# Linear attention and two feed-forward layers on one core: k and v on 128 rows in four steps and one, two attention banks in turn, q loaded a pair ahead

## The chip, the cores and the metric

The kernel runs on one core of a Trainium2 chip. The metric is the device time of one execution in microseconds (us). Before the change the median of three runs is 881.73 us (879.92 to 881.73).

## The reference, cut to what matters

q, k and v have 4 batches, 8 heads, 576 tokens and a head size of 64. Each head's kv is a sum over its 576 tokens; q times kv is normalised per token; then come two layers of the same form (512 to 2048 to 512) with different activations. All is float32.

```python
def _attn_ref(q, k, v, g_norm):
    kv = np.einsum('bhsd,bhse->bhde', k, v)
    out = np.einsum('bhsd,bhde->bhse', q, kv)
    rms = np.sqrt(np.mean(out * out, axis=-1, keepdims=True) + 1e-06)
    return (out / rms * g_norm).astype(np.float32)

def reference(...):
    x = attn_out.transpose(0, 2, 1, 3).reshape(2304, 512)
    h = x @ w_in;  sp = log1p(exp(h));  x = (h * np.tanh(sp)) @ w_out          # layer 1: mish
    h = x @ w_in2; x = (np.maximum(h, 0) + alpha * np.minimum(h, 0)) @ w_out2  # layer 2: prelu
    return x
```

## The kernel before, in words

**Blocks and slots.** The 2304 tokens are cut into five blocks (512, 256, 512, 512, 512). Each block goes through layer 1 and later through layer 2; the 2048 inner features are cut into 16 tiles, so the program has 2 x 5 x 16 = 160 slots, each for one block and one tile. In slot s TensorE does mm1(s), the product x times w_in for that tile, into a bank "h" of PSUM, and mm2(s-4), the product of the activated tile of four slots before with w_out, into four banks acc0 to acc3 that add up over the 16 tiles. Each product of two float32 values is made as three products of a high and a low part (`three`, L118 to L120): high with high, high with low, low with high. In between, mish (L458, ScalarE) or prelu (L466, L468, VectorE) reads bank h, and g_split (L451, L452) cuts the result into its parts. PSUM has eight banks; three of them are for h (`ps_h`), one is for the attention ("at").

**Weights.** The weights lie in memory as 64-bit numbers. A tile of w_in (w1) or w_out (w2) is loaded into a ring of three stage buffers "ws" (L328, L331), ScalarE scales its high words (L339), VectorE puts a float32 together from the bits (L345, L346, L349), ScalarE casts it to the high part (L384), and VectorE takes the low part (L388). In layer 1 this goes on in slots 4 to 19, one tile of w1 and one of w2 a slot.

**Attention.** Heads go in pairs, four pairs a block. The attention of block 0 stands at the start in an order written out by hand (`START`). That of the other blocks is spread over the slots before they are needed, in "hooks": hook 2s comes behind mm1(s), hook 2s+1 at the end of slot s. `WHEN[i] = (h0, step, dk, do, dm, db)` gives the places for block i: at h0 + p * step the transposes of q of pair p (t_pe, bank "tps", copied by ScalarE), dk later the sum over tokens of k times v (kv_pe, bank "kvps", where the next batch is needed), do later q times kv (o_pe, bank "ops"); after the last pair, dm later, the mean square (ms_pe) and four parts of an inverse square root on VectorE whose last result is "yr"; and from db later on, one a hook, four products that spread yr over the rows (b_pe, bank "bps", L293), each followed by VectorE's product (L299, into "qT") and the split into the parts xh and xl of x (L309, L314). Blocks 1 to 4 need kv of batches 1, 2 and 3 besides batch 0; a new batch's k and v are loaded pair by pair with q.

**kv.** k and v of a pair are loaded as 96 rows: row p holds tokens 6p to 6p+5 of both heads (`KVJ` = 6). kv_pe runs six steps, each with one product of 96 rows for each head.

**Order.** Up to slot 19 the order on every engine is the order of the program text; from slot 20 on only TensorE's is, and a scheduler places the rest. All loads are issued by SyncE (SP), in one queue. A load is called in `pre` of a slot: weights two slots and attention some slots ahead of use; in one slot the weights of the list come first. SyncE stops at a load whose buffer isn't free yet.

Of the kernel before, what the change touches and what calls it, by code (L numbers as in the profile page):

```python
# [9 lines left out]
F32 = mybir.dt.float32  # L10
# [14 lines left out]
P = 128  # L25
# [1 line left out]
EPS = 1e-6  # L27
SHIFT = 28
MAGIC = 0x5F3759DF
KVJ = 6  # L30
BLOCKS = (512, 256, 512, 512, 512)
ORDER2 = (0, 2, 3, 4, 1)
SPREAD = 4
EARLY = 4
WHEN = {1: (8, 3, 1, 2, 3, 4), 2: (-4, 4, 1, 2, 3, 7), 3: (0, 5, 1, 2, 4, 5), 4: (0, 5, 1, 2, 4, 5)}
MANUAL = 20
FIRST = "p0 c0 p1 c1 p2 p3 c2 c3 w4 u0 w5 u1".split()
START = """
# [8 lines left out]
def attn_moe_moe2(  # L47
# [27 lines left out]
    nc = tc.nc  # L75
    B, H, S, D = q.shape
# [20 lines left out]
    kvp = ctx.enter_context(tc.tile_pool(name="kvp", bufs=1))  # L97
    dp = ctx.enter_context(tc.tile_pool(name="dp", bufs=1, space=bass.MemoryType.DRAM))
    ps_acc = ctx.enter_context(tc.tile_pool(name="ps_acc", bufs=1, space=bass.MemoryType.PSUM))
    ps_h = ctx.enter_context(tc.tile_pool(name="ps_h", bufs=3, space=bass.MemoryType.PSUM))  # L100
    ps_a = ctx.enter_context(tc.tile_pool(name="ps_a", bufs=1, space=bass.MemoryType.PSUM))

    ident = const.tile([P, P], F32, name="ident")
# [39 lines left out]
    def load_kv(b, p):
        R = S // KVJ
        for nm, src in (("k", k), ("v", v)):
            cols = 2 * KVJ * D
            t = room(nm, F32, cols) if b == 0 else kvp.tile([P, cols], F32, tag=nm, name=nm)
            t = t.rearrange("p (h j d) -> p h j d", h=2, j=KVJ)
            nc.sync.dma_start(
                out=t[:R], in_=src[b, 2 * p : 2 * p + 2, :, :].rearrange("h (p j) d -> p h j d", j=KVJ)  # L150
            )
            kvt[nm, b, p] = t[:R]

    def parts(i):

# [8 lines left out]
    def load_q(i, p):  # L164
# [9 lines left out]
                )  # L174
        qt[i, p] = t

    def bank(tag, nm):
        pool = {"h": ps_h, "at": ps_a}.get(tag, ps_acc)
        return pool.tile([P, 512], F32, tag=tag, name=nm)

    def kv_pe(b, p, tag="at"):
        kt, vt = kvt.pop(("k", b, p)), kvt.pop(("v", b, p))
        ps = bank(tag, "kvps")
        for j in range(KVJ):
            for h in range(2):
                hs = slice(h * D, (h + 1) * D)
                nc.tensor.matmul(ps[hs, hs], kt[:, h, j, :], vt[:, h, j, :], start=(j == 0), stop=(j == KVJ - 1))  # L187
        at["kv", b, p] = ps

    def kv_of(b, p):  # L190
# [10 lines left out]
    def t_pe(i, p, tag="at"):  # L201
        t = qt.pop((i, p))
        ps = bank(tag, "tps")
        for c in range(BLOCKS[i] // P):
            cs = slice(c * P, (c + 1) * P)
            if i == 0:
                for h in range(2):
                    nc.tensor.matmul(ps[h * D : (h + 1) * D, cs], t[:, h, c, :], ident, start=True, stop=True)
            else:
                nc.tensor.transpose(ps[:, cs], t[:, :, c, :], ident)  # L210
        at["t", i, p] = ps
# [27 lines left out]
        nc.scalar.activation(out=sq, in_=ps, func=AF.Square)  # L239

    def m_pe(p):
        at["m", p] = bank("at", "mps")
        nc.tensor.matmul(at["m", p], ones_bd, at["o", 0, p][1], start=True, stop=True)

    def m_ev(p):
        y = at["o", 0, p][1]
        u = at["u", p] = buf(True, p, ap, TM, F32, "u", "u")
        nc.scalar.activation(
# [161 lines left out]
    hps, gs, gt, acc = {}, {}, {}, {}  # L410

    def at_slot(kk):
        b = order[kk // NJ]
        return kk // NS, b, kk % NJ, BLOCKS[b % NB]

    def mm1(kk, chunks=range(4)):
        L, i, j, T = at_slot(kk)
        if chunks[0] == 0:
            hps[kk] = bank("acc3" if kk == 3 else "h", "h")
        ps = hps[kk]  # L420
        wh, wl = w1[L, j]
# [80 lines left out]
    pre, hook, mid, fin, last = ({} for _ in range(5))  # L502

    def add(d, s, f, *a):
        d.setdefault(s, []).append((f, a))
# [2 lines left out]
        for f, a in d.pop(s, []):  # L508
            f(*a)

    early_w = [({"w": 1, "u": 2}[n[0]], int(n[1:])) for n in FIRST if n[0] in "wu"]
    for j in range(NJ):
        if j >= EARLY and (1, j) not in early_w:
            add(pre, j - 2, load_w, 0, 1, j)
            add(mid, j - 2, w_begin, 0, 1, j)
        if (2, j) not in early_w:
            add(pre, j + 2, load_w, 0, 2, j)
            add(last, j + 2, w_begin, 0, 2, j)
            add(mid, j + 3, w_end)
        s = NS - NJ + 2 + SPREAD * j // 4  # L520
        add(pre, s, load_w, 1, 1, j)
        add(fin, s + 2, prep_w, 1, 1, j)
        s = NS + j
        add(pre, s - 1, load_w, 1, 2, j)
        add(fin, s + 1, prep_w, 1, 2, j)
    new_kv = {1: 1, 2: 2, 3: 3}
    for i in range(1, NB):
        h0, step, dk, do, dm, db = WHEN[i]
        h0 += (i - 1) * 2 * NJ
        for p in range(NP):  # L530
            h = h0 + p * step
            before = max((h - step + dk) // 2 + 1 if p else h // 2 - 2, EARLY)
            add(pre, before, load_q, i, p)
            add(hook, h, t_pe, i, p)
            add(hook, h, t_ev, i, p)
            if i in new_kv:
                add(pre, before, load_kv, new_kv[i], p)
                add(hook, h + dk, kv_pe, new_kv[i], p)
                add(hook, h + dk, kv_ev, new_kv[i], p)
            add(hook, h + do, o_pe, i, p)  # L540
            add(hook, h + do, o_ev, i, p)
        h += dm
        add(hook, h, ms_pe, i)
        for part in range(4):
            add(hook, h + part, rsqrt_ev, i, part)
        for p in range(NP):
            add(hook, h + db + p, b_pe, i, p)
            add(hook, h + db + p, b_ev, i, p)
    for pos in range(NB, 2 * NB):
# [24 lines left out]
    def warm(n):  # L574
# [30 lines left out]
    with tc.manual_schedule():  # L605
        nc.scalar.preload_act_table_set("abs_reciprocal_sqrt_and_small")
        for n in FIRST:
            if n[0] == "p":
                load_kv(0, int(n[1]))
                load_q(0, int(n[1]))  # L610
            else:
                load_w(0, code[n[0]], int(n[1:]), True)
            if n == "p1":
                for h in range(2):
                    nc.sync.dma_start(out=gcol[h * D : (h + 1) * D, :], in_=g_norm.rearrange("(p o) -> p o", o=1))
# [12 lines left out]
        for p in range(NP):  # L628
            for h in range(2):
# [49 lines left out]
```

## Time and profile before

| | before |
|---|---|
| median of three runs | 881.73 us |
| the profiled execution | 880.43 us |
| its span, first to last instruction | 878.7 us |
| TensorE matmul (PE), busy | 857.0 us (98%) |
| TensorE weight load (PEld), busy | 705.9 us (80%) |
| VectorE (DVE), busy | 443.0 us (50%) |
| ScalarE (ACT), busy | 283.1 us (32%) |
| mean granted clock of TensorE | 0.996 |

The profile shows one execution; its span is 1.7 us shorter than the execution's own time, for what lies before the first and after the last instruction. Busy shares are means over the whole span. In 40 slices of the span TensorE shows 7 to 9 tenths in the first six and then 9 in all but the last; VectorE shows 5 to 9 in the first six and otherwise mostly 1 to 7. The name in front of a `<-` in a row is the tile that is written, those behind it are read. "SPq" is the queue of SyncE's loads.

### The profile page before, as it was taken

The numbers are of one execution on the slowest core, as the hardware profiler recorded it, in microseconds if no ns is written. First come the engines' busy times: TensorE is split into PE (matmuls) and PEld (weight loads), VectorE is DVE, ScalarE is ACT, GpSimd is POOL, SyncE is SP. The second block draws the span as 40 slices with busy tenths as digits, with TensorE's granted clock in tenths as the row PEclk, the third lists the DMA queues.
The fourth block names the chain that finished last, engine by engine and source line by source line (L and its number), as shares of the span: only waits on it lengthen the run. The fifth ranks groups of instructions, "written<-read, shape, count | busy, mean of one in ns | idle before, by whom it ended". The sixth has DMA issues, their size and how long they took to land.

```text
span 878.7 us, 10843 instructions
## 1 busy us (share of the span) xinstructions
PE 857.0 (98%) x4396; PEld 705.9 (80%) x4396; DVE 443.0 (50%) x752; ACT 283.1 (32%) x521; POOL 1.4 (0%) x11
## 2 busy tenths in 40 slices
PE   7988889999999999999999999999999999999998
PEld 5667668898878877888888888888888888888897
DVE  5986864531144131625777796453344334433453
ACT  4765445434323242334554342121112111111111
POOL 0000000000000000000000000000000000000000
PEclk9999999999999999999999999999999999999999
DMA  9746644203100040004632440030002000100010
GB/s 232 221 141 199 178 140 114 88 1 101 41 13 1 12 132 1 1 24 134 202 119 96 144 163 29 0 97 1 1 0 84 1 1 0 61 1 1 1 48 24
DMA packets 50754, 62.57 MB, mean 71 GB/s; under 512 B 19729, under 2 KB 41233, under 8 KB 50705
## 3 DMA queue, kind: packets, MB, share of 16 engines
q1 hardware_dynamic: 50704, 61.89, 23.6%
q8 instruction: 34, 0.56, 0.3%
q14 instruction: 16, 0.12, 0.1%
HBM read 52.44 MB, written 9.44 MB: 70 GB/s over the span
## 4 chain that ended last, share of the span: by engine, by line
PE 92%; DVE 3%; DMA 2%; ACT 1%; SPq 1%; issue 0%; DVEq 0%
PE acc L118 15%; PE acc L120 15%; PE acc L119 15%; PE h L118 15%; PE h L120 14%; PE h L119 14%; PE ops L225 2%; PE kvps L187 1%; DMA q<-in_q_dram 1%; DMA v<-in_v_dram 1%; PE tps L210 1%; DVE wf L346 1%; DVE wf L349 1%; DVE w L388 1%; PE msps L267 0%
## 5 line engine op out<-in xcount | busy, mean ns | idle before, releaser
L452 DVE TENSOR_TENSOR gl<-n,gh 128x512 fp32r<-128x512 f32 (+1 forms) x160 | 102.0, 637 | 327.8 <-ACT gh L451 327.2
L451 ACT CAST gh<-n 128x512 fp32r<-128x512 f32 (+1 forms) x160 | 92.4, 578 | 382.3 <-PE acc L119 249.1
L118 PE MATMUL h<-xh,w 128*128 128x512 f32 (+1 forms) x480 | 179.2, 373 | 0.0
L120 PE MATMUL h<-xh,w 128*128 128x512 f32 (+1 forms) x480 | 176.9, 369 | 0.1
L119 PE MATMUL h<-xl,w 128*128 128x512 f32 (+1 forms) x480 | 176.7, 368 | 0.0
L118 PE MATMUL acc<-gh,w 128*128 128x512 f32 (+1 forms) x320 | 122.1, 382 | 1.4 <-ACT n L458 1.4
L120 PE MATMUL acc<-gh,w 128*128 128x512 f32 (+1 forms) x320 | 119.5, 373 | 0.0
L119 PE MATMUL acc<-gl,w 128*128 128x512 f32 (+1 forms) x320 | 119.2, 372 | 0.0
L118 PE MATMUL acc<-w,gh 128*128 128x512 f32 x288 | 112.2, 390 | 0.0
L119 PE MATMUL acc<-w,gh 128*128 128x512 f32 x288 | 112.2, 390 | 0.0
L120 PE MATMUL acc<-w,gl 128*128 128x512 f32 x288 | 112.0, 389 | 0.0
L118 PEld LDWEIGHTS h<-xh,w 128*128 128x128 f32 x480 | 90.4, 188 | 18.5 <-issue 3.0
L119 PEld LDWEIGHTS h<-xl,w 128*128 128x128 f32 x480 | 90.6, 189 | 15.6 <-issue 0.5
L120 PEld LDWEIGHTS h<-xh,w 128*128 128x128 f32 x480 | 90.4, 188 | 15.6 <-DVE w L388 0.5
L118 PEld LDWEIGHTS acc<-gh,w 128*128 128x128 f32 x320 | 61.2, 191 | 12.6 <-ACT n L458 1.8
L120 PEld LDWEIGHTS acc<-gh,w 128*128 128x128 f32 x320 | 61.0, 191 | 10.9 <-DVE w L388 0.3
L119 PEld LDWEIGHTS acc<-gl,w 128*128 128x128 f32 x320 | 61.1, 191 | 10.3 <-issue 0.5
L120 PEld LDWEIGHTS acc<-w,gl 128*128 128x128 f32 x288 | 54.1, 188 | 11.3
L118 PEld LDWEIGHTS acc<-w,gh 128*128 128x128 f32 x288 | 54.2, 188 | 10.7
L119 PEld LDWEIGHTS acc<-w,gh 128*128 128x128 f32 x288 | 54.1, 188 | 10.7
L118 PE MATMUL h<-xh,w1first 128*128 128x512 f32 (+1 forms) x160 | 59.9, 374 | 0.0
L120 PE MATMUL h<-xh,w1first 128*128 128x512 f32 (+1 forms) x160 | 58.9, 368 | 0.0
(82 smaller groups left out, 829.0 us busy)
## 6 DMA issues: line engine op xcount, KB each, us to landing
ws<-in_moe_w_in_dram SPq DMA_DIRECT2D x32, 512.0 KB, 4.3
ws<-in_moe_w_out_dram SPq DMA_DIRECT2D x32, 512.0 KB, 3.8
k<-in_k_dram SPq DMA_DIRECT2D x16, 288.0 KB, 3.8
v<-in_v_dram SPq DMA_DIRECT2D x16, 288.0 KB, 4.3
out_dram<-osb SPq DMA_DIRECT2D x18, 256.0 KB, 2.1
x2d<-xs SPq DMA_DIRECT2D x8, 512.0 KB, 2.8
xs<-x2d SPq DMA_DIRECT2D x8, 512.0 KB, 4.0
q<-in_q_dram SPq DMA_DIRECT2D x16, 128.0 KB, 3.4
```

The costliest lines, as they stand in the source:

```text
L118: nc.tensor.matmul(ps, lh, rh, start=start, stop=False)
L119: nc.tensor.matmul(ps, lh, rl, start=False, stop=False)
L120: nc.tensor.matmul(ps, ll, rh, start=False, stop=stop)
L187: nc.tensor.matmul(ps[hs, hs], kt[:, h, j, :], vt[:, h, j, :], start=(j == 0), stop=(j == KVJ - 1))
L210: nc.tensor.transpose(ps[:, cs], t[:, :, c, :], ident)
L225: nc.tensor.matmul(cols(ps), kv_of(b, p), cols(qT), start=True, stop=True)
L346: nc.vector.scalar_tensor_tensor(out=si, in0=high, scalar=-0x80000000, in1=si, op0=ALU.bitwise_and, op1=ALU.bitwise_or)
L349: nc.vector.scalar_tensor_tensor(out=si, in0=high, scalar=3, in1=si, op0=ALU.logical_shift_left, op1=ALU.bitwise_or)
L388: nc.vector.tensor_tensor(out=l, in0=s, in1=f32(h), op=ALU.subtract)
L451: nc.scalar.copy(out=gh, in_=g)
L452: nc.vector.tensor_tensor(out=gl, in0=g, in1=f32(gh), op=ALU.subtract)
```

## The change

Five edits. k and v of a pair are loaded as 128 rows that hold tokens 4p to 4p+3 of both heads (`KVJ` = 4, the first 512 tokens) and as two loads of 64 rows for the last 64 tokens, head 0 on rows 0 to 63 and head 1 on rows 64 to 127; kv_pe has four steps of 128 rows and one of 64. The attention has two banks, at0 and at1, in turn; `ps_h` has two buffers instead of three, m_pe of the start takes at0, and mm1(2) takes at1. q of pair p+1 is loaded right behind k and v of pair p, and no longer just ahead of k and v of its own pair. In `pre` the attention's loads stand ahead of the weights', and weights are loaded three slots ahead instead of two. Last, db of block 1 goes from 4 to 6.

```diff
-KVJ = 6
+KVJ = 4
-WHEN = {1: (8, 3, 1, 2, 3, 4), ...
+WHEN = {1: (8, 3, 1, 2, 3, 6), ...
-    ps_h = ... tc.tile_pool(name="ps_h", bufs=3, space=bass.MemoryType.PSUM))
+    ps_h = ... tc.tile_pool(name="ps_h", bufs=2, space=bass.MemoryType.PSUM))
     def load_kv(b, p):
-        R = S // KVJ
+        n, m = 2 * KVJ * D, P * KVJ
         for nm, src in (("k", k), ("v", v)):
...
+            whole = t[:, :n].rearrange("p (h j d) -> p h j d", h=2, j=KVJ)
+            nc.sync.dma_start(out=whole, in_=pair[:, :m, :].rearrange("h (p j) d -> p h j d", j=KVJ))
+            for h in range(2):
+                nc.sync.dma_start(out=t[h * D : (h + 1) * D, n:], in_=pair[h, m:, :])
+            kvt[nm, b, p] = whole, t[:, n:]
+    turn = [0]
     def bank(tag, nm):
-        pool = {"h": ps_h, "at": ps_a}.get(tag, ps_acc)
+        if tag == "at":
+            turn[0] += 1
+            tag = f"at{turn[0] % 2}"
+        pool = ps_h if tag == "h" else ps_a if tag[:2] == "at" else ps_acc
     def kv_pe(b, p, tag="at"):
-        for j in range(KVJ):
+        for j in range(KVJ + 1):
...
+                kj, vj = (kt[:, h, j, :], vt[:, h, j, :]) if j < KVJ else (kr[hs], vr[hs])
+                nc.tensor.matmul(ps[hs, hs], kj, vj, start=(j == 0), stop=(j == KVJ))
     def m_pe(p):
-        at["m", p] = bank("at", "mps")
+        at["m", p] = bank("at0", "mps")
     def mm1(kk, chunks=range(4)):
-            hps[kk] = bank("acc3" if kk == 3 else "h", "h")
+            hps[kk] = bank({2: "at1", 3: "acc3"}.get(kk, "h"), "h")
...
-            add(pre, before, load_q, i, p)
+            if p == 0:
+                add(pre, before, load_q, i, p)
+            if i in new_kv:
+                add(pre, before, load_kv, new_kv[i], p)
+            if p < NP - 1:
+                add(pre, before, load_q, i, p + 1)
...
-            add(pre, j - 2, load_w, 0, 1, j)
+            add(pre, max(j - 3, EARLY), load_w, 0, 1, j)
-            add(pre, j + 2, load_w, 0, 2, j)
+            add(pre, max(j + 1, EARLY), load_w, 0, 2, j)
```

The loop that adds the weights' loads moves behind the one that adds the attention's.

SyncE's queue, at the loads of k and v of block 1's pair 2. Before, where q_730 is q of the same pair:

```order
L331 DMA ws_728<-in_moe_w_in_dram 128x4x256
L171 DMA q_730<-in_q_dram 32x2x64 x2
L171 DMA q_730<-in_q_dram 96x2x64 x2
L149 DMA k_735<-in_k_dram 96x2x384
L149 DMA v_737<-in_v_dram 96x2x384
L328 DMA ws_806<-in_moe_w_out_dram 128x1024
```

The same place now, where q_610 is q of pair 2 and q_755 that of pair 3:

```order
L173 DMA q_610<-in_q_dram 32x2x64 x2
L173 DMA q_610<-in_q_dram 96x2x64 x2
L336 DMA ws_615<-in_moe_w_out_dram 128x1024
L339 DMA ws_617<-in_moe_w_in_dram 128x4x256
L336 DMA ws_677<-in_moe_w_out_dram 128x1024
L339 DMA ws_679<-in_moe_w_in_dram 128x4x256
L151 DMA k_747<-in_k_dram 128x2x256
L153 DMA k_747<-in_k_dram 64x64 x2
L151 DMA v_751<-in_v_dram 128x2x256
L153 DMA v_751<-in_v_dram 64x64 x2
L173 DMA q_755<-in_q_dram 32x2x64 x2
L173 DMA q_755<-in_q_dram 96x2x64 x2
```

q of pair 2 has moved four weight loads ahead of k and v of pair 2; those two have become six loads, and they stand behind the same number of weight loads as before (eight from slot 4 on).

VectorE, around the first b product of block 1 (qT_528 before, qT_549 now), w113 being the low part of w1 tile 13, w114 that of tile 14 and w29 that of w2 tile 9. Before:

```order
L388 TENSOR_TENSOR w113_1067<-wf_1036,w113_1067 128x512
L299 SCALAR_TENSOR_TENSOR qT_528<-o_612,gcol_95,bps_1096 128x256
L314 TENSOR_TENSOR xl0_1100<-qT_528,xh0_1099 128x256
L388 TENSOR_TENSOR w29_1105<-wf_1063,w29_1105 128x512
L345 TENSOR_SCALAR wf_1109<-ws_1072 128x512
```

Now:

```order
L396 TENSOR_TENSOR w113_1087<-wf_1056,w113_1087 128x512
L396 TENSOR_TENSOR w29_1127<-wf_1083,w29_1127 128x512
L353 TENSOR_SCALAR wf_1131<-ws_1032 128x512
L354 SCALAR_TENSOR_TENSOR wf_1131<-ws_1032,wf_1131 128x512
L357 SCALAR_TENSOR_TENSOR wf_1131<-ws_1032,wf_1131 128x512
L460 TENSOR_TENSOR gl_1148<-n_1050,gh_1147 128x512
L396 TENSOR_TENSOR w114_1156<-wf_1131,w114_1156 128x512
L307 SCALAR_TENSOR_TENSOR qT_549<-o_635,gcol_95,bps_1174 128x256
L322 TENSOR_TENSOR xl0_1178<-qT_549,xh0_1177 128x256
```

The b product and its split have moved from between the low parts of w1 tile 13 and w2 tile 9 to behind that of w1 tile 14; on TensorE the product itself has moved from behind mm1(12) to behind mm1(13).

ScalarE, around mish(12), the row with h_1083 before and h_1112 now. Before:

```order
L309 CAST xh1_1132<-qT_644 128x256
L339 ACTIVATE ws_1070<-ws_1070 128x512
L384 CAST w114_1141<-wf_1109 128x512
L309 CAST xh2_1164<-qT_755 128x256
L458 ACTIVATE n_1168<-h_1083 128x512
```

Now:

```order
L459 CAST gh_1147<-n_1050 128x512
L347 ACTIVATE ws_1030<-ws_1030 128x512
L392 CAST w114_1156<-wf_1131 128x512
L317 CAST xh0_1177<-qT_549 128x256
L466 ACTIVATE n_1181<-h_1112 128x512
L392 CAST w210_1183<-wf_1152 128x512
```

mish(12) stood behind the casts of the second and third xh; now it stands behind that of the first.

## Rows read from the trace of the kernel before

**Rows 1.** Stretches: us; PE, PEld, DVE, ACT, POOL busy (count); PEclk, DMA share, GB/s.

```profile
0.00:40.00 40.00, 33.87 (x254) 23.93 (x254) 29.48 (x78) 22.74 (x37) 1.43 (x11) 1.00 0.95 249
40.00:125.00 85.00, 73.65 (x398) 56.88 (x397) 69.20 (x124) 46.57 (x94) 0.00 (x0) 0.96 0.54 157
430.00:520.00 90.00, 90.00 (x398) 74.55 (x398) 69.62 (x116) 41.53 (x72) 0.00 (x0) 1.00 0.43 140
```

**Rows 2.** Waits of TensorE, 0 to 170 us: total us, times, longest.

```profile
PE bps L293 <- DVE yr L287: 3.6, 1, 3.6
PE tps L210 <- DMA q<-in_q_dram: 2.8, 1, 2.8
PE tps L210 <- DVE qT L299: 1.9, 1, 1.9
...
PE kvps L187 <- DMA v<-in_v_dram: 1.6, 2, 1.1
...
PE acc L118 <- ACT n L458: 1.4, 1, 1.4
```

**Rows 3.** Stretches in the start and behind the wait for yr, as Rows 1.

```profile
10.00:15.00 5.00, 3.66 (x47) 2.37 (x45) 2.52 (x5) 2.52 (x5) 0.00 (x0) 1.00 1.09 244
20.00:25.00 5.00, 4.23 (x46) 2.44 (x48) 4.35 (x8) 3.28 (x7) 0.00 (x0) 1.00 1.05 353
105.00:106.00 1.00, 1.00 (x4) 0.81 (x3) 0.97 (x2) 0.00 (x0) 0.00 (x0) 0.50 1.02 192
```

**Rows 4.** The chain that ended last, 0 to 25 us: start us, us, what.

```profile
0.73 0.39 SPq L149
...
3.10 0.43 SPq L149
3.57 8.10 DMA v<-in_v_dram
...
12.08 7.88 DMA q<-in_q_dram
```

**Rows 5.** DMA issues: count, KB each, median us from issue to landing.

```profile
v<-in_v_dram SPq DMA_DIRECT2D x16, 288.0 KB, 4.3
...
q<-in_q_dram SPq DMA_DIRECT2D x16, 16.0 KB, 3.4
```

**Rows 6.** Timeline of SyncE's queue: start us, us, what, and how many.

```profile
63.55 0.38 SPq L331 DMA_DIRECT2D ws<-in_moe_w_in_dram  x1
63.98 2.50 SPq L171 DMA_DIRECT2D q<-in_q_dram  x4
```

**Rows 7.** Timeline of TensorE.

```profile
71.48 0.92 PE L187 MATMUL kvps<-v,k 96*64 96x64 f32 x24
72.33 0.50 PE L118 MATMUL h<-xh,w 128*128 128x512 f32 x1
...
109.09 0.40 PE L118 MATMUL h<-xh,w 128*128 128x512 f32 x1
...
126.75 0.50 PE L118 MATMUL h<-xh,w 128*128 128x512 f32 x1
...
514.14 0.39 PE L118 MATMUL h<-xh,w 128*128 128x512 f32 x1
```

**Rows 8.** Timeline of VectorE; in brackets idle us before and what ended it.

```profile
70.22 0.69 DVE L388 TENSOR_TENSOR w<-wf,w 128x512 fp32r<-128x512 f32 x1 [3.70 <-ACT w L384]
...
106.05 0.69 DVE L388 TENSOR_TENSOR w<-wf,w 128x512 fp32r<-128x512 f32 x1
...
108.61 0.69 DVE L388 TENSOR_TENSOR w<-wf,w 128x512 fp32r<-128x512 f32 x1 [0.58 <-ACT w L384]
...
123.60 1.46 DVE L388 TENSOR_TENSOR w<-wf,w 128x512 fp32r<-128x512 f32 x2
...
514.33 0.68 DVE L468 SCALAR_TENSOR_TENSOR n<-h,n 128x512 f32<-128x512 f32 x1
```

**Rows 9.** Costliest groups: busy us, mean ns of one, idle before.

```profile
L451 ACT CAST gh<-n 128x512 fp32r<-128x512 f32 (+1 forms) x160 | 92.4, 578 | 382.3 <-PE acc L119 249.1
```

More of the change, by code (lines that the diff above doesn't have):

```diff
@@ L34 @@
 EARLY = 4
-WHEN = {1: (8, 3, 1, 2, 3, 4), 2: (-4, 4, 1, 2, 3, 7), 3: (0, 5, 1, 2, 4, 5), 4: (0, 5, 1, 2, 4, 5)}
+WHEN = {1: (8, 3, 1, 2, 3, 6), 2: (-4, 4, 1, 2, 3, 7), 3: (0, 5, 1, 2, 4, 5), 4: (0, 5, 1, 2, 4, 5)}
 MANUAL = 20
@@ L83, in attn_moe_moe2 @@
     NB = len(BLOCKS)
+    assert S == P * KVJ + D and 2 * D == P
     TM = max(BLOCKS)
@@ L99, in attn_moe_moe2 @@
     ps_acc = ctx.enter_context(tc.tile_pool(name="ps_acc", bufs=1, space=bass.MemoryType.PSUM))
-    ps_h = ctx.enter_context(tc.tile_pool(name="ps_h", bufs=3, space=bass.MemoryType.PSUM))
+    ps_h = ctx.enter_context(tc.tile_pool(name="ps_h", bufs=2, space=bass.MemoryType.PSUM))
     ps_a = ctx.enter_context(tc.tile_pool(name="ps_a", bufs=1, space=bass.MemoryType.PSUM))
@@ L143, in load_kv @@
     def load_kv(b, p):
-        R = S // KVJ
+        n, m = 2 * KVJ * D, P * KVJ
         for nm, src in (("k", k), ("v", v)):
[L146 to L152, printed above, removed]
+            t = room(nm, F32, n + D) if b == 0 else kvp.tile([P, n + D], F32, tag=nm, name=nm)
+            pair = src[b, 2 * p : 2 * p + 2, :, :]
+            whole = t[:, :n].rearrange("p (h j d) -> p h j d", h=2, j=KVJ)
[3 more added lines that the diff above has]
+            kvt[nm, b, p] = whole, t[:, n:]
     def parts(i):
@@ L175, in load_q @@
         qt[i, p] = t
+    turn = [0]
     def bank(tag, nm):
-        pool = {"h": ps_h, "at": ps_a}.get(tag, ps_acc)
+        if tag == "at":
+            turn[0] += 1
+            tag = f"at{turn[0] % 2}"
+        pool = ps_h if tag == "h" else ps_a if tag[:2] == "at" else ps_acc
         return pool.tile([P, 512], F32, tag=tag, name=nm)
     def kv_pe(b, p, tag="at"):
-        kt, vt = kvt.pop(("k", b, p)), kvt.pop(("v", b, p))
+        (kt, kr), (vt, vr) = kvt.pop(("k", b, p)), kvt.pop(("v", b, p))
         ps = bank(tag, "kvps")
-        for j in range(KVJ):
+        for j in range(KVJ + 1):
             for h in range(2):
                 hs = slice(h * D, (h + 1) * D)
-                nc.tensor.matmul(ps[hs, hs], kt[:, h, j, :], vt[:, h, j, :], start=(j == 0), stop=(j == KVJ - 1))
+                kj, vj = (kt[:, h, j, :], vt[:, h, j, :]) if j < KVJ else (kr[hs], vr[hs])
+                nc.tensor.matmul(ps[hs, hs], kj, vj, start=(j == 0), stop=(j == KVJ))
         at["kv", b, p] = ps
@@ L509, in run @@
             f(*a)
-    early_w = [({"w": 1, "u": 2}[n[0]], int(n[1:])) for n in FIRST if n[0] in "wu"]
-    for j in range(NJ):
-        if j >= EARLY and (1, j) not in early_w:
-            add(pre, j - 2, load_w, 0, 1, j)
-            add(mid, j - 2, w_begin, 0, 1, j)
-        if (2, j) not in early_w:
-            add(pre, j + 2, load_w, 0, 2, j)
[L518 to L525, printed above, removed]
     new_kv = {1: 1, 2: 2, 3: 3}
@@ L536, in attn_moe_moe2 @@
             if i in new_kv:
-                add(pre, before, load_kv, new_kv[i], p)
                 add(hook, h + dk, kv_pe, new_kv[i], p)
@@ L548, in attn_moe_moe2 @@
             add(hook, h + db + p, b_ev, i, p)
+    early_w = [({"w": 1, "u": 2}[n[0]], int(n[1:])) for n in FIRST if n[0] in "wu"]
+    for j in range(NJ):
+        if j >= EARLY and (1, j) not in early_w:
+            add(pre, max(j - 3, EARLY), load_w, 0, 1, j)
+            add(mid, j - 2, w_begin, 0, 1, j)
+        if (2, j) not in early_w:
+            add(pre, max(j + 1, EARLY), load_w, 0, 2, j)
+            add(last, j + 2, w_begin, 0, 2, j)
+            add(mid, j + 3, w_end)
+        s = NS - NJ + 2 + SPREAD * j // 4
+        add(pre, s, load_w, 1, 1, j)
+        add(fin, s + 2, prep_w, 1, 1, j)
+        s = NS + j
+        add(pre, s - 1, load_w, 1, 2, j)
+        add(fin, s + 1, prep_w, 1, 2, j)
     for pos in range(NB, 2 * NB):
```

## The prediction

> **What bounds the kernel now.** I read busy time by stretch first. From 40 to 125 us TensorE is busy 73.65 of 85.00 us while VectorE is busy 69.20; from 430 to 520 TensorE has no idle time [rows 1], and the waits say nearly nothing after 170 us. So after about 125 us a microsecond is only won by giving TensorE less to do, and before that by taking waits away. The waits of TensorE up to 170 us name them: 3.6 us for yr, 2.8 us for a q load, 1.9 us for the bank that the last of the four b products of block 1 holds, 1.6 us for v at the start, and 1.4 us before the fourth accumulator of the first mm2, for mish(3) [rows 2]. Third, the clock: 0.96 on average from 40 to 125 [rows 1] and 0.50 from 105 to 106 [rows 3], right after the 3.6 us wait for yr; (1 - 0.96) x 85 / 0.5 gives some 6.8 us at the lower level of 1.2 GHz, in which half the work is lost: 3.4 us. Fourth, the chain and the DMA windows for the start: v of pair 1 takes 8.10 us from issue to landing, q of pair 2 7.88 [rows 4], with the DMA engines' share above 1 at 244 GB/s where 96-row k and v loads flow, but 353 GB/s from 20 to 25, where weights flow on 128 rows [rows 3].
>
> **The start (0 to 47 us).** What is added: six DMAs for a pair of k and v instead of two, at 0.43 us of issue each [rows 4]. q of pair 2 becomes DMA number 28, so it can't be issued before 0.73 + 27 x 0.45 = 12.9 us, against 12.08 now: 0.8 us later or more. What is changed: the loads now fill all 128 rows. If their rate goes from 244 towards 353 GB/s, the 7.88 us from issue to landing shrink to 3.4 (the landing time of a small q load without a crowd [rows 5]) to 5, and q of pair 2 lands at 16.3 to 18 instead of 19.96. The two waits for v (1.6 us together) go as well. VectorE then starts its dense stretch (from 18 us on) about 2 us earlier, and everything up to 47 us hangs on it. Bounds: if the rate stays at 244 GB/s and the issues count in full, 2 us later; if TensorE's and VectorE's idle time before 20 us shrinks by all the DMA waits, 3.5 us earlier. I take 2.0 us earlier, since in these microseconds the load and not the issue is what lands last. The Trainium skill, SBUF — State Buffer, section "Door 1: The DMA port swizzle", says that rows 0 to 63 reach only half of the ports and rows 64 to 127 the other half, so that 96 rows load one half twice as much as the other; by it the loads speed up and the term is a gain of 2 to 3.5; the trace agrees as far as 244 against 353 GB/s go.
>
> The first transpose of block 1 now takes the bank that kk 2 holds until mish(2), about 1 us after TensorE gets there. That costs nothing while the wait for mish(3), three products later (1.4 us [rows 2]), is still there to swallow it.
>
> **The q loads (52 to 100 us).** q of block 1, pair 2 is issued at 63.98, after a weight load at 63.55 that had waited for its stage buffer [rows 6]; its four issues last until 66.48, and the transpose waits 2.84 us for it [rows 2]. In the new order this q comes a pair earlier and k, v of pair 2 stand where q stood. The q wait goes. Next late is v: six issues from 63.98 on end near 66.7; a whole k or v lands 4.3 us after issue and a 16 KB piece 3.4 us [rows 5], so v is complete at 65.3 + 4.3 or 66.3 + 3.4, about 69.7. TensorE would start that kvps at 71.48 - 2.84 = 68.6 [rows 7]. So some 1 us of the 2.84 comes back at the kvps. VectorE gains nearly all of it: its 3.70 us of idle time before 70.22 [rows 8] end with a ScalarE cast that is queued behind the copy of that transpose. The weight loads, asked for one slot earlier, change nothing by themselves: k and v of pair 2 have eight of them ahead in SyncE's order before and after, and each waits for a stage buffer as now. I take VectorE 2.8 us earlier from 70 us on; the weight ring (a load starts when the buffer three loads back is used) moves along with it.
>
> **The b products (100 to 127 us).** With db 6 instead of 4, TensorE doesn't stop for yr; it runs mm2(8) and stops at mm1(13), whose third product wants the low part of w1 tile 13. VectorE has it at 106.05 + 0.69 = 106.7 now [rows 8], 2.8 earlier: 103.9. TensorE's third product of mm1(13) is at 109.09 + 0.47 = 109.6 now [rows 7]. So the place of the yr wait is taken by a wait for the weights, and still 5.6 us are won there, because the mm2(8) that ran after the wait, and at half clock, now lies before it. Behind it, VectorE no longer has the first two products' work between the low parts: the first took 108.61 - 106.05 less one pitch of 0.60 = 1.96, the second the same less its 0.6 wait, 1.3 us. Tile 15's low part, 123.60 + 0.69 = 124.3 now [rows 8], comes 2.8 + 3.2 = 6.0 earlier, at 118.3. mm1(15) also needs mish(13) out of its bank, which sits on ScalarE behind the third xh and a transpose copy: with some four operations of 0.58 us [rows 9] to run there, about 118.3 + 2.4 = 120.7 against 126.75 now [rows 7]. Two attention banks: b product 3 needs the bank of product 1, long read, and the transpose of block 2 that of product 2 instead of the last; the wait of 1.9 becomes about 1.3. Two h banks instead of three: mm1(14) now waits for mish(12), which is queued on ScalarE behind the first xh, for about 1.5 us; that lies inside the slack that mm1(15) has until 120.7. Together, 40 to 127: 5.6 us won, taking the smaller of the two ends of the chain. Bounds: 2.3 won (only the q wait less what comes back less 0.5 of new bank waits), and 11 (all of TensorE's 11.35 us of idle time in the stretch but a little).
>
> **The kv products.** 24 of them take 0.85 us a pair (71.48 to 72.33 [rows 7]); 20 take 0.71: 0.14 less. But the last step works on 64 rows: the first product after a kvps takes 0.50 us and not 0.39 [rows 7], so a change of shape shows as 0.11. One more of it leaves 0.03 a pair, 0.4 us over the 12 pairs behind the start. Ends: the two tail products side by side, 0.21 a pair, 2.5 us won; two more changes, 0.08 a pair, 1.0 lost. I take the value nearest to the 0.11 row. The Trainium skill, TensorEngine Tiling (Array Packing), section "Key Properties", says that changing the tiling mode drains TensorE; by it the 0.11 is paid and the sum stays; without it the kv term would be 1.7.
>
> **Two h banks later on.** For each slot I set the release of the bank two slots back against the start of its mm1. Of the slots from 21 on two would have waited: slot 88, at 514.14, for a release at 514.33 + 0.68 = 515.0 [rows 7, 8], 0.9 us; slot 74 0.6 us. Both lie where weights of layer 2 are prepared and VectorE is busy 69.62 of 90 us [rows 1]. I take 1.0 us lost; ends 0 and 4 (35 slots, 73 to 92 and 145 to 159, have slack under 2.4 us, many under 1).
>
> Sum, against the profiled execution's 880.43: 880.43 - 2.0 - 5.6 - 0.4 + 1.0 = 873.4. The median of the three runs, 881.73, stands 1.3 above the profiled one; I name 874.
>
> **Rivals.**
> More DMAs, nothing faster (chance 0.13): the rate of the loads stays, eight loads in flight are now smaller ones, and the start ends 2 us later; the kvps of pair 2 waits another 0.5. 880.4 + 2.0 - 5.1 - 0.4 + 1.0 = 877.9. For it: 0.43 us an issue, and SyncE's issue already waits for older loads in the start. Against it: the share of the DMA engines is above 1, so the queue is full anyway.
> The waits move and nothing is won (0.08): VectorE at 69.20 of 85 us sets the pace of 40 to 125, its work is unchanged, and the wait for tile 13 is as long as the one for yr. 880 to 881. Against it: the 3.70 us of idle time are VectorE's own.
> More than forecast (0.10): start -3.5, kv -2.0, the h banks 0, 40 to 127 -6.5: 868.4.
> Two h banks decide (0.07, the slower side): mm1 of each of the 35 slots of slack under 2.4 us waits for a release that VectorE and ScalarE, in a new order, give later. At 0.24 us a slot (8.4 in all) the gain without the h term is gone; at 0.5 a slot it is 872.4 + 17.5 = 890. Against it: two slots only where the trace has it.
> The forecast has 0.62.
>
> **How the numbers follow.** A difference under 0.2% (1.8 us) can't be told from none here. Faster is the forecast, the first rival and the third: 0.62 + 0.13 + 0.10 = 0.85; the same 0.08; slower 0.07. The range from 868 to 879 holds the forecast with its own spread (870 to 877) and the two rivals on its side, and leaves 0.15 outside.
>
> **What would show it.** Right: no wait of a transpose of block 1 for q; v of pair 2 landing at 69 to 70 with a short wait of the kvps; a wait of mm1(13) for a low part in place of the one for yr; no clock of 0.50 for as long as 6.8 us; the first x of block 1 at mm1(16) some 7 to 8 us earlier; k and v loads at above 300 GB/s in the start; a kvps of about 0.8 us. Wrong: the first dense stretch of VectorE no earlier than 18 us; a wait of mm1 for mish in many slots; the gain of 40 to 127 under 3 us.

## The result and the profile after

The change makes the kernel slower: 886.52 us (median of six runs, 885.41 to 890.42) against 880.97. The ratio on record, which is not that of the two medians (1.0063), is 1.0077 (95% interval 1.0063 to 1.0091). The profiled execution took 886.76 us, with a span of 885.0 and a mean granted clock of 0.988. The forecast was 874.0.

Busy time by stretch of the changed kernel, with the columns of [rows 1, 3]:

```profile
0.00:40.00 40.00, 33.61 (x225) 23.34 (x226) 26.91 (x74) 20.19 (x32) 1.43 (x11) 0.91 0.69 204
40.00:125.00 85.00, 74.11 (x383) 57.28 (x382) 67.10 (x119) 45.48 (x93) 0.00 (x0) 0.95 0.56 173
...
10.00:15.00 5.00, 4.23 (x44) 2.53 (x42) 2.95 (x6) 2.98 (x5) 0.00 (x0) 1.00 0.56 160
20.00:25.00 5.00, 4.22 (x23) 2.23 (x21) 4.20 (x8) 1.90 (x3) 0.00 (x0) 0.54 0.71 190
```

From 10 to 15 us the DMA engines are now busy for 0.56 of the time and move 160 GB/s, where they were full at 244 [rows 3]: the loads don't saturate them any more. From 20 to 25 us the clock is near 1.2 GHz (0.54), where it was 1.00. The waits of TensorE up to 170 us:

```profile
PE kvps L195 <- DMA v<-in_v_dram: 5.9, 3, 3.5
PE tps L218 <- DVE qT L307: 3.3, 1, 3.3
PE h L119 <- ACT n L466: 2.3, 2, 1.8
...
PE h L121 <- DVE w L396: 0.4, 1, 0.4
```

The waits for yr (3.6 us) and for q (2.8) of [rows 2] are gone. In their place stand waits for v, for the bank of a b product, for mish and a short one for a low part.

Where the time went is read best from the start of mm1 in some slots, that is, from the first product into h on TensorE's timeline. The first column is the time before in us; the others are differences to it. Each column is one profiled execution; e4 leaves out the tails, the last 64 tokens of k and v, so its kv sums over 512 of the 576 tokens:

| mm1 of slot | before | changed | e4, no tails | e5, tails on GpSimd | e8, e5 with old banks | e9, tails once a batch | e12, e9 + h banks + db 4 |
|---|---|---|---|---|---|---|---|
| 0 | 25.81 | +3.05 | -2.50 | +4.85 | +3.86 | +0.13 | -0.89 |
| 7 | 62.48 | +2.51 | -3.57 | +4.27 | +3.31 | -0.43 | -1.44 |
| 9 | 79.02 | +4.29 | -5.79 | +2.18 | +1.13 | -2.68 | -3.71 |
| 12 | 97.92 | +4.29 | -6.01 | +2.22 | +1.17 | -2.64 | -3.70 |
| 13 | 109.09 | +0.57 | -9.65 | -1.49 | -3.03 | -6.34 | -4.67 |
| 14 | 116.18 | +1.92 | -8.29 | -0.14 | -1.33 | -4.99 | -2.98 |
| 16 | 133.24 | +4.85 | -9.48 | -1.08 | +6.29 | -2.78 | -3.63 |
| 72 | 427.10 | +4.97 | -11.17 | -0.95 | +6.48 | -2.66 | -3.50 |
| 159 | 866.52 | +6.32 | -9.33 | +0.99 | +6.48 | -0.85 | -3.51 |

So the changed kernel loses 3.05 us in the start and 1.80 between slots 0 and 16, and 1.35 after slot 72. Part of this is the clock: TensorE was at the lower level four times between 17 and 131 us, where the kernel before was twice, around 105 and 122 us. It is not the main part: of the six executions of the changed kernel the one with the highest mean clock, 0.998, took 885.41 us.

**The start.** SyncE's queue for the first pair, start and length of the issues:

```profile
0.73 0.45 SPq L151 DMA_DIRECT2D k<-in_k_dram  x1
1.24 1.20 SPq L153 DMA_DIRECT2D k<-in_k_dram  x2
2.48 0.59 SPq L151 DMA_DIRECT2D v<-in_v_dram  x1
3.11 1.12 SPq L153 DMA_DIRECT2D v<-in_v_dram  x2
4.27 1.06 SPq L173 DMA_DIRECT2D q<-in_q_dram  x2
5.37 0.43 SPq L341 DMA_DIRECT2D ws<-in_moe_w_in_dram  x1
...
12.65 0.43 SPq L151 DMA_DIRECT2D k<-in_k_dram  x1
...
15.17 0.59 SPq L151 DMA_DIRECT2D v<-in_v_dram  x1
15.80 1.12 SPq L153 DMA_DIRECT2D v<-in_v_dram  x2
16.97 1.06 SPq L173 DMA_DIRECT2D q<-in_q_dram  x2
```

k of the second pair is issued at 5.85 us instead of 3.10 [rows 4], and the last issue for v of pair 2 ends at 16.92. Pairs count from 0, so this is the third. TensorE has been idle since 16.91 and waits for it; then the clock is down:

```profile
18.66 1.53 PE L195 MATMUL kvps<-v,k 128*64 128x64 f32 x20 [1.75 <-DMA v<-in_v_dram]
20.13 2.07 PE L251 MATMUL mps<-q,ones_bd 128*128 128x512 f32 x2
22.13 1.98 PE L216 MATMUL tps<-ident,q 128*64 128x128 f32 x16
```

The same two mps products take 1.12 us at the upper level (at 12.69 us of this trace); here they take 2.07. The three rows together take 5.58 us, against 3.16 for the same three at the upper level (0.95, 1.12 and 1.09, from 11.81 us on).

**Slots 7 and 8.** SyncE's queue ahead of k and v of block 1's pair 2, and TensorE's wait behind it:

```profile
53.38 0.45 SPq L151 DMA_DIRECT2D k<-in_k_dram  x1
53.87 1.15 SPq L153 DMA_DIRECT2D k<-in_k_dram  x2
55.07 0.59 SPq L151 DMA_DIRECT2D v<-in_v_dram  x1
55.70 1.11 SPq L153 DMA_DIRECT2D v<-in_v_dram  x2
56.85 2.53 SPq L173 DMA_DIRECT2D q<-in_q_dram  x4
...
60.53 0.37 SPq L339 DMA_DIRECT2D ws<-in_moe_w_in_dram  x1
...
68.62 0.37 SPq L339 DMA_DIRECT2D ws<-in_moe_w_in_dram  x1
...
71.42 1.11 SPq L153 DMA_DIRECT2D v<-in_v_dram  x2
```

```profile
74.52 0.95 PE L195 MATMUL kvps<-v,k 128*64 128x64 f32 x20 [3.52 <-DMA v<-in_v_dram]
```

Ten issues (k, v and q) fill the queue from 53.38 to 59.38, so the two weight loads behind them go out only at 59.51 and 60.53. VectorE then stands idle for the second, and the stage buffer that SyncE waits for comes free late:

```profile
66.48 0.43 DVE L353 TENSOR_SCALAR wf<-ws 128x512 int32<-128x512 int32 x1 [2.32 <-DMA ws<-in_moe_w_in_dram]
```

That is 5.95 us after its issue, so it was also slow to land; the same load of the kernel before was issued at 56.47 and landed 4.69 us later. The weight load ahead of k and v, issued at 63.55 before the change [rows 6], goes out at 68.62, and the products with v start only at 74.5. Behind the wait the clock falls, which it didn't behind the wait of 2.84 us for q before the change:

```profile
74.00:80.00 6.00, 5.48 (x34) 4.42 (x35) 3.79 (x7) 1.59 (x4) 0.00 (x0) 0.72 0.69 208
```

How much this place costs changes from one execution to the next. e1 and e13 (below) have the old loads and the same program up to there; the one loses 3.2 us from slot 7 to 9, the other wins 1.2:

```profile
70.18 1.55 PE L192 MATMUL kvps<-v,k 96*64 96x64 f32 x24 [3.71 <-DMA v<-in_v_dram]
```

```profile
68.78 0.92 PE L193 MATMUL kvps<-v,k 96*64 96x64 f32 x24 [2.14 <-DMA v<-in_v_dram]
```

e11, with the tails on SyncE there, wins 1.1. So the loss at this place can't be put down to the tail loads by these traces.

**Slots 13 and 14.** The order of events is the same at block 2's first pair: from 106.24 to 115.72 SyncE issues q, k, v and the next q, and the weight load behind them makes VectorE wait. First VectorE, then TensorE:

```profile
121.33 0.43 DVE L353 TENSOR_SCALAR wf<-ws 128x512 int32<-128x512 int32 x1 [2.05 <-DMA ws<-in_moe_w_in_dram]
...
123.97 0.47 DVE L307 SCALAR_TENSOR_TENSOR qT<-o,gcol,bps 128x256 f32<-128x256 f32 x1
```

```profile
109.66 0.55 PE L119 MATMUL h<-xh,w 128*128 128x512 f32 x1 [1.84 <-ACT n L466]
...
111.07 0.79 PE L121 MATMUL h<-xh,w 128*128 128x512 f32 x1 [0.44 <-DVE w L396]
...
124.50 1.11 PE L218 MATMUL tps<-ident,q 128*128 128x128 f32 x4 [3.25 <-DVE qT L307]
```

The b product's qT that frees the bank for block 2's transpose is queued on VectorE behind that weight tile.

### The profile page after: what moved, and what is told of

Its sections match the earlier page's. It is cut to its first block, busy times and chain, and to the rows that moved or that the text cites. A ratio compares the mean times of both kernels' runs of the same rounds, so it can differ in the third digit from the quotient of the medians.

```text
span 885.0 us, 10780 instructions
## 1 busy us (share of the span) xinstructions
PE 862.8 (97%) x4332; PEld 708.8 (80%) x4332; DVE 443.0 (50%) x752; ACT 283.3 (32%) x521; POOL 1.4 (0%) x11
## 4 chain that ended last, share of the span: by engine, by line
PE 89%; DMA 3%; DVE 3%; SPq 2%; ACT 1%; issue 1%; DVEq 0%
PE h L119 14%; PE acc L119 14%; PE acc L120 14%; PE acc L121 14%; PE h L121 14%; PE h L120 14%; PE ops L233 2%; PE kvps L195 1%; DMA ws<-in_moe_w_in_dram 1%; SPq L153 1%; DMA v<-in_v_dram 1%; SPq L173 1%; PE tps L218 1%; DVE wf L357 1%; DMA k<-in_k_dram 1%
## 5 line engine op out<-in xcount | busy, mean ns | idle before, releaser
L119 PE MATMUL h<-xh,w1first 128*128 128x512 f32 (+1 forms) x160 | 59.9, 374 | 0.0
L120 PE MATMUL h<-xl,w1first 128*128 128x512 f32 (+1 forms) x160 | 58.9, 368 | 0.0
```

## The experiments

Theory A: what costs is the number of loads in SyncE's queue. Theory B: the bytes of the tails land late, whoever issues them. Theory C: the banks. Medians, and ratios on record to the kernel before, each beside its own runs of it:

| run | edit | us | ratio (95%) |
|---|---|---|---|
| e1 | changed, old k and v loads and products | 877.21 | 0.9975 (0.9958 to 0.9992) |
| e2 | before, new k and v loads and products | 886.31 | 1.0072 (1.0054 to 1.0091) |
| e3 | changed, tails issued by GpSimd | 888.00 | 1.0090 (1.0071 to 1.0109) |
| e4 | changed, no tails at all | 870.55 | 0.9893 (0.9874 to 0.9911) |
| e5 | e3, identity ahead of the loads | 881.89 | 1.0015 (1.0005 to 1.0025) |
| e6 | e4 with four one-row loads a pair | 879.71 | 0.9995 (0.9981 to 1.0009) |
| e7 | changed, one tail load for both heads | 885.85 | 1.0062 (1.0045 to 1.0078) |
| e8 | e5 with the old banks | 887.88 | 1.0075 (1.0054 to 1.0096) |
| e9 | changed, tails loaded once a batch | 879.29 | 0.9982 (0.9968 to 0.9997) |
| e10 | e9, four h banks from slot 68 on | 877.38 | 0.9961 (0.9946 to 0.9975) |
| e11 | changed, old loads in the start alone | 881.60 | 1.0020 (1.0002 to 1.0038) |
| e12 | e10, db of block 1 back at 4 | 875.70 | 0.9938 (0.9922 to 0.9954) |
| e13 | e1, four h banks from slot 68 on, db 4 | 875.92 | 0.9956 (0.9939 to 0.9973) |
| e14 | e12, q ahead of k, v of its own pair | 879.89 | 0.9993 (0.9978 to 1.0009) |

**The load edit alone, and the rest alone (e1, e2).** e1 puts back `load_kv` and `kv_pe`, e2 moves just these two into the kernel before:

```diff
-KVJ = 4
+KVJ = 6
```

> The changed kernel with k and v loaded and multiplied as before (96 rows, six steps, two loads a pair); all other edits stay. Theory A (issue: four more loads a pair at some 0.57 us each on SyncE's queue push back every load behind them): mm1(0) starts at 25.8 us as before the change instead of 28.9, the kvps of block 1, pair 2 doesn't wait 3.5 us for v, and the gains of the other edits show: 875 to 878 us. Theory B (transfer: the 64-row loads of 256-byte runs land late, whoever issues them): the same 875 to 878. Theory C (banks: two banks for h and two in turn for the attention cost more than the loads): only the start's 3 us come back, 882 to 884, and the waits of slots 13 to 15 stay.

> The kernel before with the new k and v loads and kv products alone (four steps of 128 rows and one of 64, six loads a pair). A and B: start 3 us later, the q load of block 1, pair 2 and with it the transpose later still, since q stands ahead of k and v but behind the former pair's: 885 to 888 us. C: 883 to 884, the start alone.

C's 882 to 884 is out. e1's mm1(0) is at 24.20, with the old loads 1.6 us earlier than before the change: the other edits win this much in the start. A wait of 3.71 us for v of pair 2 stayed in its profiled execution (880.35 us, one of its slower half; 87 us from 40 on at a mean clock of 0.92), which A had not expected. e2 is as slow as the whole change: the loss is in the load edit. The two don't add up, though: the other edits win 2.9 us with the old loads and nothing with the new ones.

**The tails off SyncE (e3, e5).**

```diff
-                nc.sync.dma_start(out=t[h * D : (h + 1) * D, n:], in_=pair[h, m:, :])
+                nc.gpsimd.dma_start(out=t[h * D : (h + 1) * D, n:], in_=pair[h, m:, :])
```

> The changed kernel with the 64-row loads issued by GpSimd, which has nothing else to do, instead of SyncE; the same bytes and the same runs. A: the start comes back (mm1(0) at 25 to 26.5), no long wait for v of pair 2: 875 to 879. B: the loads land as late as in the changed kernel, 885 to 888. C: 882 to 884.

> As the kernel with the 64-row loads on GpSimd, but GpSimd makes the identity matrix and clears the kv tiles before its first load, where in that kernel they stood behind eight loads and held up the first transpose (7.8 us). A (issue on SyncE): mm1(0) at 23 to 27 us instead of 35.7, the middle as in that kernel (5.7 us won from mm1(0) to mm1(16)): 873 to 879 us. B (the 64-row loads land late whoever issues them): mm1(0) at 28 to 29 and 884 or more.

e3 missed A's range in part for a reason of its own: GpSimd's text order put the identity behind sixteen tail loads and the first transpose waited 7.8 us, until 16.79. The identity was made at 12.57; what the rest of the wait was for the trace doesn't show. GpSimd's timeline in e3:

```profile
10.94 1.05 POOL L153 DMA_DIRECT2D v<-in_v_dram  x2
11.96 0.25 POOL masks.py:197 MEMSET ident<- 128x128 f32 x1
```

e5 mends that, and its mm1(0) is 5.0 us earlier. Its 881.89 us lie between A's range and B's, and mm1(0), at 30.66, lies behind both. From slot 0 to 16 e5 wins 5.9 us (from +4.85 to -1.08), where the changed kernel loses 1.8, with the same bytes, as A has it. The start is against A: its first tails land late too, as TensorE's timeline in e5 shows, and from 10 to 15 us the clock is 0.57.

```profile
9.24 0.29 PE L195 MATMUL kvps<-v,k 64*64 64x64 f32 x2 [2.56 <-DMA v<-in_v_dram]
10.98 0.44 PE L195 MATMUL kvps<-v,k 64*64 64x64 f32 x2 [1.44 <-DMA v<-in_v_dram]
```

**No tails, and loads nearly without bytes (e4, e6).** e4 takes out the two lines that load the tails and the fifth step; e6 adds to e4 (neither sums kv over the last 64 tokens):

```diff
+            for x in range(2):
+                nc.sync.dma_start(out=t[x * D : x * D + 1, n:], in_=pair[x, m : m + 1, :])
```

> The changed kernel without the 64-row loads and without the fifth step of the kv products, so kv is summed over 512 of 576 tokens; two loads of 128 rows a pair. A and B: 874 to 878. C: 882 to 884. Beside that it gives the price of the fifth step: a pair's kv products take 0.87 us in the changed kernel; if the products are paid by their number, 16 of them take 0.70.

> The changed kernel without the 64-row loads and the fifth step (kv is summed over 512 of 576 tokens), but with four loads of a single row of 256 bytes in their place on SyncE, which nothing reads. A: the place in the queue is what costs, so the time is that of the changed kernel less the fifth step's some 2 us: 881 to 886. B: the bytes are what costs, so it is that of the kernel without tails, 870 to 872.

Four one-row loads a pair, read by nobody, cost 9.2 us (870.55 to 879.71). That is more than half of the 16.0 between e4 and the changed kernel (886.52), and it is far from B's 870 to 872. It is 1.3 below A's range, so A is not all. e4 itself came 3.5 us below the range that A and B shared.

e4's start shows what the 128-row loads are worth. Its stretch from 10 to 15 us, and a kv product of it with the product behind:

```profile
10.00:15.00 5.00, 3.73 (x40) 2.34 (x39) 3.54 (x8) 3.00 (x5) 0.00 (x0) 1.00 0.96 324
```

```profile
216.89 0.69 PE L193 MATMUL kvps<-v,k 128*64 128x64 f32 x16
217.51 0.50 PE L119 MATMUL h<-xh,w 128*128 128x512 f32 x1
```

324 GB/s instead of 244 before the change (278 in e1, with the old loads and the other edits), and 16 products in 217.51 - 216.89 = 0.62 us, where 0.70 was expected. At mm1(0) e4 is 0.9 us ahead of e1.

**Fewer loads for the same bytes (e7, e9).**

```diff
-            for h in range(2):
-                nc.sync.dma_start(out=t[h * D : (h + 1) * D, n:], in_=pair[h, m:, :])
+            nc.sync.dma_start(out=t[:, n:], in_=pair[:, m:, :])
```

e9 loads, at pair 0 of a batch, the tails of all four pairs:

```diff
+            rest = src[b].rearrange("(p h) s d -> h s p d", h=2)[:, m:]
+            for h in range(2):
+                nc.sync.dma_start(out=t[h * D : (h + 1) * D].rearrange("s (p d) -> s p d", d=D), in_=rest[h])
```

> The changed kernel with the two 64-row loads of k as one load of 128 rows, and so for v: four loads a pair instead of six, the same bytes. A: half of the added issues go, so about half of the loss against the kernel without tails (16 us): 876 to 881, with a start 0.5 to 1 us later than before the change. B: the bytes and runs are the same, 884 to 887.

> The changed kernel with the last 64 tokens of k and v loaded once a batch instead of once a pair: four loads of 64 rows with four runs of 256 bytes on each row, for all four pairs, so the same bytes and the same runs, but 12 loads a batch instead of 24, all on SyncE. A (the number of loads in SyncE's queue): near the kernel without tails (870.6) plus the fifth step's 2 us and the four loads ahead of pair 0: 873 to 877. B (bytes and runs of the tails): 883 to 887, as the changed kernel. A third, A2 (what a pair waits for is the last landing, and only the start counts): 878 to 881.

e7 missed A's range and lies in B's: 0.7 us won where about 8 were expected. Its start is even later (mm1(0) at 30.56), with two waits for v of 1.6 and 2.3 us. Its queue has fewer issues, but one of them holds SyncE for 4.23 us, from 6.83 on, and the next goes out at 11.11; what it waits for there the trace doesn't show:

```profile
6.83 4.71 SPq L172 DMA_DIRECT2D q<-in_q_dram  x2
```

Yet between slots 0 and 16 e7 wins 0.8, where the changed kernel loses 1.8. e9 has 12 loads of k and v a batch instead of 24 and is 7.2 us faster than the changed kernel, but 2 us above A's range. It lies in the range of the third reading, by which only the start counts; but it also wins 2.9 us between slots 0 and 16 (+0.13 to -2.78), so that reading falls too. Its kv products split into the steps of 128 rows and the fifth:

```profile
12.91 0.69 PE L203 MATMUL kvps<-v,k 128*64 128x64 f32 x16 [1.16 <-DMA v<-in_v_dram]
13.53 0.33 PE L203 MATMUL kvps<-vr,kr 64*64 64x64 f32 x4
13.79 1.12 PE L259 MATMUL mps<-q,ones_bd 128*128 128x512 f32 x2
```

0.62 us for sixteen, 0.26 for four.

**The banks (e8, e10).** e8 undoes the banks in e5; e10 adds to e9 from slot 68 on, with `LATE` = 68:

```diff
-            hps[kk] = bank({2: "at1", 3: "acc3"}.get(kk, "h"), "h")
+            hps[kk] = bank({2: "at1", 3: "acc3"}.get(kk, f"at{kk % 2}" if kk >= LATE and kk // 2 % 2 else "h"), "h")
```

> As the kernel with the 64-row loads on GpSimd and the identity first, with the banks as before the change (three for h, one for the attention). If two h banks cost what slots 72 to 159 show (1.4 to 2.5 us in five traces), those come back; against that the b products of block 1 and the transpose of block 2 take turns in one bank again (2.8 us of waits before the change). A and B: within 2 us of that kernel. C (banks cost more than loads): 3 us or more below it.

> As the kernel with the tails loaded once a batch, and from slot 68 on, when the attention is done, its two banks serve h in turn with the two of h, so four. The waits of mm1 for a bank in slots 72 to 159 (1.4 to 2.0 us from slot 72 to 159 in the traces with two) go: 1.4 to 2.0 below that kernel. If they are not bank waits: the same.

Both bounds of e8 fell on the other side: the old banks lose 6.0 us. Five of its six executions ran at a mean clock of 0.988; the sixth, at 0.996, took 882.69, 0.8 us more than e5. So most of the 6.0 hangs on the clock, which in the profiled execution fell behind these waits (0.81 from 104 to 140 us, 0.95 in e5). Waits of TensorE in e8 up to 170 us:

```profile
PE tps L215 <- DVE qT L304: 3.4, 1, 3.4
...
PE kvps L192 <- DVE qT L304: 1.7, 1, 1.7
...
PE bps L298 <- DVE qT L304: 1.3, 1, 1.3
```

From slot 14 to 16 e8 loses 7.6 us (-1.33 to +6.29), e5 wins 0.9; from slot 72 on e8 loses nothing and e5 1.9. e10 gets that back: 1.9 us, as expected.

**The start alone, db and q (e11, e12, e14).** e11 keeps the old loads for batch 0, e12 sets `WHEN[1]` to (8, 3, 1, 2, 3, 4) in e10, and e14 moves the call of `load_q` back in e12.

> The changed kernel with k and v of batch 0 alone as before the change (96 rows, six steps, two loads a pair), later batches with 128 rows and tails. A: the start is as before the change (mm1(0) at 24 to 26 us, 3 to 5 us earlier than in the changed kernel), the middle loses as there, since its loads are the same: 881 to 884. If the middle's loss only follows from the late start: 875 to 877.

> As the kernel with batched tails and four h banks late, with db of block 1 back at 4. The product for the first x of block 1 then stands right behind mm1(12) again and waits for yr, some 3 to 4 us with a lower clock behind it: 3 to 5 us above that kernel. If the two attention banks alone make the middle faster and the place of the product doesn't matter: the same within 1 us.

> As the kernel with batched tails, four h banks late and db 4, but q of a pair is loaded ahead of k and v of its own pair, as before the change. If the q loads a pair ahead win the 2.8 us of the wait for q: 877.5 to 879. If what is won at the transpose is given back at the kvps: the same within 1 us of 875.7.

e11: by the medians 4.9 us below the changed kernel, and in the traces 4.4 at mm1(0) (24.45). The median is in A's range, but in the profiled execution, its second fastest of twelve (879.60), the middle doesn't lose as A had it: it wins 1.7 from slot 0 to 16. So part of the changed kernel's loss there seems to follow from the late start; slower executions of e11 have no trace. e12 has the wait for yr back (3.6 us) and is still 1.7 us faster than e10: db 6 doesn't win, against both readings. With db 6, block 2's transpose waits 3.5 us in e10 for the bank of a b product; with db 4 this wait is gone, and one of 2.8 us for mish stands in slot 14. e14 loses 4.2 us, 0.9 more than its range has; TensorE's waits in e14 name it:

```profile
PE tps L227 <- DMA q<-in_q_dram: 3.9, 1, 3.9
```

**Without the split (e13).** e1 with the edits of e10 and e12:

> k and v as before the change (96 rows, six steps, two loads a pair), with two attention banks in turn, q a pair ahead, four h banks from slot 68 on and db 4. If the split is worth nothing: 877.2 (the same with db 6 and two h banks) less 1.9 for the h banks and 1.7 for db, 873.6, so 872 to 875. If the 128-row loads are what keeps the kvps of pair 2 from waiting: 876 to 879, above the kernel with batched tails (875.7).

Its median is e12's within 0.3 us, and the intervals overlap; it lies between the two expected ranges. So the split into 128 rows and a tail has no gain left that these runs can tell, even with few loads; e12 and e13 both beat the kernel before and the changed one.

## Why the prediction was wrong

**The start, forecast -2.0, measured +3.05.** The step that failed is "since in these microseconds the load and not the issue is what lands last". Of the first half of the reasoning a part held: 128 rows load faster (324 GB/s from 10 to 15 us in e4, 278 in e1). The Trainium skill, SBUF — State Buffer, section "Door 1: The DMA port swizzle", has rows 0 to 63 on one half of the ports and rows 64 to 127 on the other; e4's 324 GB/s agree with it. But even with no issue added that was worth 0.9 us at mm1(0) (e4 against e1) and not 2.0. And the issue did come last: q of pair 2 was to go out at 12.9, at 0.45 us a load, and went at 16.97 behind 26 others, 0.62 a load. The DMA engines were busy for 0.56 of the time from 10 to 15 us, so the premise of the full queue ("the share of the DMA engines is above 1, so the queue is full anyway") fell. I had put the late issue at the bound of 2 us. Behind the wait of 1.75 us the three groups up to 24.1 us ran 2.4 us longer at the lower clock, and the sum went past that end. Against e1 and e11, which keep the old loads there, the new loads cost the start 4.4 to 4.7 us; the 1.6 that the other edits win there was in no term.

**The q loads, forecast -1.8 net, measured +1.8 (slots 7 to 9).** q a pair ahead did its part and more: undone, it costs 4.2 us (e14). The failed step is that v of pair 2 is complete "about 69.7". I counted six issues behind a weight load at 63.55, and forgot that the former pair's issues stand ahead of the weight load: with the start 3.05 later it should have gone out at 66.6 and went at 68.62, behind VectorE's wait of 2.32 us for a weight load that was late behind the ten issues from 53.38 on and slow to land. The products with v started at 74.5. So some 1 us was to come back as a wait for v, and 3.52 came; it is 3.71 and 2.14 with the old loads (e1, e13). The lower clock behind it, (1 - 0.72) x 6 = 1.7 us, was in no term.

**The b products, forecast -3.8 or so of the 5.6, measured +0.6 (slots 12 to 16).** The wait for yr goes and a wait for mish and a low part comes, as forecast: mm1(13) gains 3.7. It is given back at block 2's transpose, for which I forecast a wait of 1.3 and which waits 3.25, for VectorE, which waits for a weight load that stands behind block 2's first loads. The kernels with db 6, two attention banks and no tail loads on SyncE at that place (e1, e3, e4, e5) win 3.0 to 3.5 us from slot 12 to 16; of those with tails there the changed kernel, e9, e10 and e11 win 0.1 at most or lose up to 0.6, and e7 wins 1.2. e6, with as many loads there as the changed kernel but hardly any bytes in the added ones, wins 2.8, so the number of loads alone doesn't explain this place; each of these figures is from one execution. The move to db 6, on which I rested the gain, is worth less than nothing where the tails stand there (e12 against e10: 1.7 us); two attention banks do help (e8: 6.0 us by the medians, 0.8 where the clock stayed up).

**The kv products, forecast -0.4, measured some +0.3**: 0.88 us a pair (74.52 to 75.40) instead of 0.85, over twelve pairs. The mis-sized term is the products of 128 rows: sixteen were to take 16/24 of 0.85, that is 0.57, and take 0.62, 39 ns each against 35 of 96 rows. The fifth step was right: 0.14 + 0.11 = 0.25 forecast, 0.26 measured in e9. The Trainium skill, TensorEngine Tiling (Array Packing), section "Key Properties", has TensorE drain at a change of the tiling mode. The four products of 64 rows take 0.10 us more than four of 39 ns would, which agrees with it; no run separates a drain from slower products.

**Two h banks, forecast +1.0, measured +1.35** after slot 72, and undone in e10 for 1.9. This term was right.

The first rival, more DMAs and nothing faster, named the mechanism in part (eight loads in flight that are now smaller ones); but its 877.9 lay 4.5 us above the sum of 873.4, and the profiled execution lies 13.4 above it. It left out what stands behind the loads in the queue: the weights.

How the 16.0 us between e4 and the changed kernel divide: 9.2 for four more loads a pair (e6); some 4 for the fifth step, if all sixteen pairs pay its 0.26; the other 2 to 3 stay open. Why a load counts is open in part. In the traces that record landings SyncE never has more than eight loads between issue and landing: the ninth waits for the first. In e6, whose one-row loads take half the time to issue, this wait is what holds the start. SyncE's timeline in e6, then two of its waits up to 20 us:

```profile
5.99 0.61 SPq L153 DMA_DIRECT2D v<-in_v_dram  x2
7.89 2.11 SPq L173 DMA_DIRECT2D q<-in_q_dram  x2
...
12.20 0.43 SPq L151 DMA_DIRECT2D k<-in_k_dram  x1
```

```profile
SPq L173 <- DMA ws<-in_moe_w_in_dram: 3.1, 2, 1.7
SPq L173 <- DMA q<-in_q_dram: 1.3, 1, 1.3
```

k of pair 2 goes out at 12.20 there and at 12.65 in the changed kernel, against 9.25 in e4. So a load takes one of eight places, however small it is, and the DMA engines have less to do beside it (0.52 from 10 to 15 us in e6, 0.96 in e4). In the changed kernel's start SyncE waits only 0.7 us in this way; there its own issuing fills the time. e7, with half the added loads but the same pieces, fits neither, and its stop of 4.23 us stays open.

## What to carry to other kernels

A load that is split costs its place in the issuing queue, and whoever stands behind it pays: count the issues from the previous pair on, up to the load that the critical engine wants, and ask what stage buffer or earlier landing each waits for. Here the gain in load rate showed only where the DMA engines were kept full (0.96 in e4, 0.56 in the changed kernel). Pieces too small for a load of their own are loaded for several users at once (e9), and two attention banks in turn paid more here than a third h bank, which can be had back when the attention is over (e10). A wait in one trace is one execution: e1 and e13 differ by 4.4 us at a place where their programs are the same.

## What the runs showed of the hardware

A load of a single row of 256 bytes still takes SyncE 0.31 us to issue (two in 0.62, e6); one of 64 rows takes 0.56 on SyncE (two in 1.12) and 0.52 on GpSimd (two in 1.05). Executions of one kernel differ with the clock: e11's at a mean granted clock of 0.992 or less took 881.75 to 888.36 us, those at 0.994 or more 879.52 to 881.87. In the start, a wait of 1.16 us (e9) left the clock at 1.00 and one of 1.75 (the changed kernel) was followed by 0.54 from 20 to 25 us; but a wait of 2.84 before the change, up to 68.37, left it at 1.00 (68 to 75 us), so the length of the wait alone doesn't tell. In every trace that records landings at most eight loads of one queue, SyncE's or GpSimd's, are between issue and landing.
